# Fused attention and snake MLP on one core: the start of batch 0 regrouped by halves of its heads, and its loads reordered

## The chip, the cores and the metric

The kernel runs on one core of a Trainium2 chip. The metric is device time in microseconds for one launch, inputs and output in the chip's memory. Engines are named as the profile names them: PE is the matrix engine (PEld its weight loads), DVE is VectorE, ACT is ScalarE, POOL is GpSimd, SP is SyncE, which here only issues DMAs. DMAs are issued from the queues of SP, ACT and POOL and run on 16 shared DMA engines.

## The reference

Two stages. A linear attention over 8 batches, 8 heads, 576 tokens and a head dimension of 64, and then a feed-forward layer with a snake activation on the 4608 tokens of width 512.

```python
q_s = np.exp(q - q.max(-1, keepdims=True)); q_s /= q_s.sum(-1, keepdims=True) + 1e-09   # over the head dimension
k_s = np.exp(k - k.max(2, keepdims=True));  k_s /= k_s.sum(2, keepdims=True) + 1e-09    # over the tokens
kv  = np.einsum('bhsd,bhse->bhde', k_s, v)
x   = np.einsum('bhsd,bhde->bhse', q_s, kv)      # -> [4608, 512]
h = x @ w_in                                     # w_in [512, 2048]
s = np.sin(alpha * h)
out = (h + s * s / (alpha + 1e-09)) @ w_out      # w_out [2048, 512]
```

The kernel leaves out the subtraction of the maximum and the small constants, and works in bf16 between f32 inputs and an f32 output.

## The kernel before, in words

**Attention.** One batch is loaded as three tiles of [128, 4, 9, 64] in f32, for q, k and v: a partition is a pair (e, p), head parity and token group; i counts the four pairs of heads; j is one of 9 tokens of a group. A half ii of the heads is the pairs i = ii and ii + 2. Per batch: ACT takes exp of q and k (`exp_q`, `exp_k`, L117); DVE sums and normalises q to qn (`norm_q`, L144 to L146); PE transposes qn to qT (`q_transpose_ii`, L186; DMA transposes in later batches); v is cast to bf16 beside a column of ones (`cast_v0`, L310, for batch 0); PE multiplies k by v over the tokens (`kv_mm`, L157, 18 small matmuls per half); DVE divides by the sums that the column of ones gave, and writes a block-diagonal kbd (`kv_norm`, L167 and L170); PE multiplies kbd by qT (`attn_chunk`, L214), and the result, evacuated from PSUM, is xT, with chunk c of its four belonging to half c // 2.

**Feed-forward.** The 4608 tokens are nine tiles t of 512. For each t and each of 16 column blocks ni, PE computes h from four chunks ki of w_in and xT (`mm_h`, L234), ACT takes the sine (L240), one of ACT, DVE and POOL squares it (L242, L246, L244, by a letter string), and DVE combines s, 1/alpha and h to g in bf16 (`combine`, L250). Then PE multiplies g by w_out (`mm_o`, L254, 64 matmuls of 512 columns per t in four accumulators), and the results are copied (L260) and stored.

**Order.** The order of instructions on each engine is the order of the program text: it is written out by hand, each engine runs its own in order, and waits are semaphores. PSUM is 8 banks: a pool `ps_h` of four one-bank buffers and, during tiles 0 and 1, a pool `ps_e` of two two-bank buffers. Both are rings: a new tile takes the buffer of the one four (or two) before it and waits for its last reader. In tiles 0 and 1 some h come from `ps_e` instead (`lent`): for t = 0 those with ni % 6 in (2, 3). So six h can be in flight.

**The start.** SP issues q and k of batch 0 in halves, v in three parts, and the first 256 columns of w_in in f32 (`st_w`), which POOL later casts to bf16 (L320). POOL waits for the first half of k (`held`, L317) and then issues the rest of w_in with a cast in the DMA, in column blocks (`load_win`, L107), and two quarters of w_out (`load_wout`, L110). PE waits for its data with matmuls that only keep it busy (`warm_up`, L306). Both halves of batch 0 go through exp, norm and transposition, then kv for both, then the four x chunks with their evacuations (L342), a sine on a dummy that loads ACT's table (L343), and h for t = 0. Token group j 8 of batch 0 belongs to tile 1; it is transposed at the start with the others, and its x is computed after ten o matmuls of tile 0 and evacuated by ACT (L393 to L396). `take(os, n)` is: issue the next n o matmuls of the tile before.

Of the kernel before, what the change touches and what calls it, by code (L numbers as in the profile page):

```python
# [23 lines left out]
def kernel(  # L24
# [14 lines left out]
    nc = tc.nc  # L39
# [36 lines left out]
    def src_view(t, b):  # L76
        return t[b].rearrange("(i e) (p j) d -> (e p) i (j d)", e=2, j=J)
# [25 lines left out]

    def load_win(c0, c1):
        n = slice(c0, c1)
        for x in range(2):
            nc.gpsimd.dma_start(out=win[64 * x:64 * x + 64, :, n], in_=win_v[x][:, :, n])  # L107

    def load_wout(c):
        nc.gpsimd.dma_start(out=wout[:, 4 * c:4 * c + 4, :], in_=wout_v[:, 4 * c:4 * c + 4, :])  # L110
# [3 lines left out]

    def exp_to(dst, src):
        for ii in range(2):
            nc.scalar.activation(dst[:, :, ii * 128:(ii + 1) * 128].rearrange("p j (x d) -> p x j d", x=2),  # L117
                                 src[:, ii::2], AX.Exp)

    def exp_q(b):  # L120
        A["qe", b] = att2.tile([128, J, 4 * D], BF16, name="qe")
        exp_to(A["qe", b], staged["q", b])

    def exp_k(b):
        A["ke", b] = att2.tile([128, J, 4 * D], BF16, name="ke")
        exp_to(A["ke", b], staged["k", b])
# [95 lines left out]
    def mm_h(t, ni, wide=None, k0=0, k1=4):  # L222
# [3 lines left out]
        if k0:  # L226
            hp = HP[t, ni]
        elif wide and ni % 6 in ((2, 3) if t == 0 else (4, 5)):
            hp = wide()
        else:  # L230
            hp = ps_h.tile([128, MF], F32, name="hp", tag="h")
# [35 lines left out]
    ACT_CP, DVE_CP, GP_CP = nc.scalar.copy, nc.vector.tensor_copy, nc.gpsimd.tensor_copy  # L267
    V, GP = nc.vector, nc.gpsimd
    nc.scalar.dma_start(out=alpha_rows, in_=moe_alpha.rearrange("(no ni) -> no ni", ni=128))
    load("q", q, 0, halves=True)  # L270
    load("k", k, 0, halves=True)
    staged["v", 0] = st = stage.tile([128, 4, J, D], F32, name="st_v", tag="st")
    VJ = ((0, 0, 9), (1, 0, 5), (1, 5, 9))
    for ii, j0, j1 in VJ:
        nc.sync.dma_start(out=st[:, ii::2, j0:j1].rearrange("p i j d -> p i (j d)"),
                          in_=src_view(v, 0)[:, ii::2, j0 * D:j1 * D])

    wf = stage.tile([128, 4, J, D], F32, name="st_w", tag="st")[:, :, 0:4].rearrange("p c a b -> p c (a b)")
    for x in range(2):
        nc.sync.dma_start(out=wf[64 * x:64 * x + 64], in_=win_v[x][:, :, 0:256])  # L280
    make_identity(nc, ident)
# [10 lines left out]

    tps = [ps_h.tile([128, 8, 128], BF16, name="tp", tag="h") for _ in range(3)]
    warm = ps_h.tile([128, 4, 128], F32, name="warm", tag="h")
# [4 lines left out]

    exp_q(0)  # L300
    exp_k(0)

# [4 lines left out]

    def cast_v0(ii, j0, j1, eng):
        vv = vb[0].rearrange("p j (i c) -> p i j c", i=4)
        eng(vv[:, 2 * ii:2 * ii + 2, j0:j1, 0:D], staged["v", 0][:, ii::2, j0:j1])  # L310


    warm_up(7)
    norm_q(0, [V, V])
    q_tile(0)

    GP_CP(singles.tile([128, 1], F32, name="held"), staged["k", 0][:, 0, 0, 0:1])  # L317
    for c0, c1 in ((256, 512), (512, 1024), (1024, 1536)):
        load_win(c0, c1)
    GP_CP(win[:, :, 0:256], wf)  # L320
    load_win(1536, 2048)
    for c in range(2):
        load_wout(c)
    q_transpose_ii(0, 0, 0, 8, tps[0])
    ACT_CP(A["qT", 0][:, 0, 0:8], tps[0])
    cast_v0(0, 0, 5, ACT_CP)
    cast_v0(0, 5, 9, DVE_CP)
    warm_up(6)
    q_transpose_ii(0, 1, 0, 8, tps[1])
    for ii in range(2):  # L330
        q_transpose_ii(0, ii, 8, 9, tps[2][:, ii:ii + 1])
    cast_v0(1, 0, 5, DVE_CP)
    cast_v0(1, 5, 9, ACT_CP)
    ACT_CP(A["qT", 0][:, 1, 0:8], tps[1])
    ACT_CP(A["qT", 0][:, :, 8], tps[2][:, 0:2])
    for ii in range(2):
        kv_mm(0, ii, ps_e, split=True)
        kv_norm(0, ii, ii + 1)
    for c in range(4):
        xp = ps_h.tile([128, MF], F32, name="hp", tag="h")  # L340
        attn_chunk(0, c, 0, 8, xp)
        (ACT_CP, DVE_CP)[c % 2](xT[:, c, 0:MF], xp)  # L342
    nc.scalar.activation(zero, zero, AX.Sin)  # L343

    def h_slot(t, ni, sq, lag, wide=None):
        hp = mm_h(t, ni, wide, 2 if t < 2 and ni < 2 else 0)
        lag.append((t, ni, hp, sine(t, ni, hp, sq)))
# [26 lines left out]
    with ES:  # L374
        def lent():
# [3 lines left out]
                10: lambda: load_wout(3), 13: lambda: load("k", k, 1, halves=True, gate=DVE_CP)}  # L379
        for ki in range(2):  # L380
            for ni in range(2):
                mm_h(0, ni, lent, ki, ki + 1)
        for ni in range(nN):
# [7 lines left out]
        os = o_quad(0, accs, [DVE_CP, ACT_CP, DVE_CP, ACT_CP])  # L391
        take(os, 10)
        xp = ps_e.tile([128, 4, P], F32, name="xp", tag="a")  # L393
        for c in range(4):
            attn_chunk(0, c, 8, 9, xp[:, c])
        ACT_CP(xT[:, :, 8 * P:9 * P], xp)  # L396
        take(os, 36)
        exp_q(1)
# [169 lines left out]
```

The softmax here doesn't subtract the row's maximum and nothing guards it: scores larger than these inputs give would overflow.

## Time and profile before

| | |
|---|---|
| time, median of 13 runs | 289.76 us (288.81 to 292.38, and one of 491.87) |
| the profiled execution, its own time | 291.86 us |
| its span in the profile | 290.1 us, 4262 instructions |
| mean clock granted to PE | 0.994 |
| first exp (ACT) / first h matmul (PE) / first sine (ACT) | 4.60 / 16.82 / 19.56 us |
| first o matmul (PE) | 32.33 us |
| HBM read and written | 36.71 and 9.44 MB |

The profile is of one execution, and times in it count from the start of its span; its own time is the span and 1.76 us around it. A row of the page is a group of instructions: line, engine, operation, output and inputs with shapes, count, busy time in all and mean of one, then the idle time just before them and what ended most of it. The chain that ended last is followed back from the last instruction.

### The profile page before, as it was taken

Reading aid. Unit: us, or ns where it says so; the run is one execution under the profiler, and the core shown is the slowest. Engines: PE = TensorE matmul, PEld = TensorE weight load, DVE = VectorE, ACT = ScalarE, POOL = GpSimd, SP = SyncE. Lnnn points to the kernel's source line nnn. Section 1 sums busy time; section 2 is a strip of 40 time slices with the busy share of each in tenths; the row PEclk is TensorE's granted clock in tenths of the full one; section 3 lists DMA queues with packets and bytes.
Section 4 is the critical chain, followed back from the end, with each engine's and each line's share of the span. In section 5 each row is a group of like instructions: output and inputs, shape, how many; then the busy total and the mean of one; then the engine's idle time right before and its main releaser. Section 6 shows DMA issues by size and latency. Waiting matters only on the chain.

```text
span 290.1 us, 4262 instructions
## 1 busy us (share of the span) xinstructions
PE 277.4 (96%) x1570; PEld 131.5 (45%) x1570; DVE 188.9 (65%) x280; ACT 227.4 (78%) x321; POOL 79.4 (27%) x73
## 2 busy tenths in 40 slices
PE   2889999999999999999999999999999999999994
PEld 1434445445454445444544454445444444444443
DVE  3847768699958667766777576747674555555412
ACT  4679776899668999899889998899887777777500
POOL 0557720567585743004400350023000000000000
PEclk9979999999999999999999999999999999999999
DMA  7999999963989969019901891115111111111142
GB/s 256 336 204 182 246 362 408 313 251 83 235 120 384 411 216 157 19 26 320 335 21 37 280 368 32 37 38 118 36 38 36 36 36 38 36 36 37 40 108 72
DMA packets 37893, 46.03 MB, mean 159 GB/s; under 512 B 15968, under 2 KB 21360, under 8 KB 37872
## 3 DMA queue, kind: packets, MB, share of 16 engines
q1 hardware_dynamic: 33392, 41.69, 47.6%
q0 software_dynamic: 4288, 3.93, 8.5%
q8 instruction: 12, 0.20, 0.3%
q10 hardware_dynamic: 192, 0.14, 0.2%
q14 instruction: 9, 0.07, 0.1%
HBM read 36.71 MB, written 9.44 MB: 159 GB/s over the span
## 4 chain that ended last, share of the span: by engine, by line
PE 83%; DMA 5%; POOL 4%; DVE 3%; SPq 1%; issue 1%; ACT 1%; POOLq 0%
PE hp L234 36%; PE op L254 34%; PE hp L254 4%; DMA st_w<-in_moe_w_in_dram 4%; POOL s L244 3%; PE kvp L157 2%; PE xp L206 2%; PE hh L234 2%; DMA qT<-qn 1%; PE op L538 1%; PE op L234 1%; ACT s L240 1%; DVE g L250 1%; DVE qs L144 1%; SPq L94 1%
## 5 line engine op out<-in xcount | busy, mean ns | idle before, releaser
L250 DVE SCALAR_TENSOR_TENSOR g<-s,inva_sb,hp 128x512 bf16<-128x512 f32 x130 | 96.2, 746 | 64.4 <-ACT s L242 54.2
L234 PE MATMUL hp<-xT,win 128*128 128x512 bf16 x520 | 131.4, 383 | 0.6 <-POOL win L320 0.6
L254 PE MATMUL op<-wout,g 128*128 128x512 bf16 x496 | 124.2, 379 | 0.0
L240 ACT ACTIVATE s<-hp,alpha_sb 128x512 f32<-128x512 f32 x130 | 87.8, 682 | 27.0 <-PE hp L234 25.8
L234 PEld LDWEIGHTS <-win 128*128 128x128 bf16 x576 | 56.7, 99 | 69.4 <-issue 2.4
L254 PEld LDWEIGHTS <-g 128*128 128x128 bf16 x560 | 54.1, 98 | 61.9 <-issue 1.0
L242 ACT ACTIVATE s<-s 128x512 f32<-128x512 f32 x112 | 70.5, 630 | 3.5
L146 POOL TENSOR_TENSOR qn<-qe,qs 128x1152 bf16<-128x1152 bf16 x12 | 25.3, 2128 | 73.8 <-DVE qs L140 62.8
L244 POOL TENSOR_TENSOR s<-s 128x512 f32<-128x512 f32 x29 | 30.5, 1061 | 24.0 <-ACT s L240 23.3
L260 DVE COPY o<-op 128x512 f32<-128x512 f32 (+2 forms) x33 | 22.1, 669 | 9.9 <-PE op L254 7.5
L117 ACT ACTIVATE ke<-st_k 128x1152 bf16<-128x1152 f32 x16 | 17.9, 1151 | 3.2 <-DMA st_k<-in_k_dram 3.2
L117 ACT ACTIVATE qe<-st_q 128x1152 bf16<-128x1152 f32 x16 | 17.8, 1156 | 2.5 <-DMA st_q<-in_q_dram 2.4
L139 DVE TENSOR_REDUCE qs<-qe 128x36 f32<-128x2304 bf16 x5 | 12.8, 2553 | 8.7 <-ACT qe L117 8.6
L131 POOL CAST vb<-st_v 128x1152 bf16<-128x1152 f32 x12 | 13.6, 1163 | 10.5 <-DMA st_v<-in_v_dram 6.9
L254 PE MATMUL hp<-wout,g 128*128 128x512 bf16 x64 | 15.1, 379 | 0.0
L209 DVE CAST xT<-xp 128x512 bf16<-128x512 f32 (+1 forms) x18 | 13.4, 743 | 0.0
L144 DVE TENSOR_REDUCE qs<-qe 128x18 f32<-128x1152 bf16 x6 | 8.0, 1331 | 4.4 <-ACT qe L117 4.4
L157 PE MATMUL kvp<-vb,ke 64*128 64x130 bf16 x288 | 10.0, 216 | 0.8 <-ACT vb L310 0.8
L157 PEld LDWEIGHTS <-ke 64*128 64x128 bf16 x288 | 8.3, 93 | 4.4 <-issue 1.8
L117 ACT ACT_TABLE_LOAD x7 | 9.0, 1283 | 1.3 <-PEq L552 1.2
L234 PE MATMUL hh<-xT,win 128*128 128x512 bf16 x40 | 9.5, 381 | 0.0
L206 PE MATMUL xp<-qT,kbd 128*128 128x256 bf16 (+1 forms) x40 | 8.2, 286 | 0.4 <-DVE xT L209 0.3
(68 smaller groups left out, 117.5 us busy)
## 6 DMA issues: line engine op xcount, KB each, us to landing
out_dram<-o SPq DMA_DIRECT2D x70, 128.0 KB, 2.4
st_q<-in_q_dram SPq DMA_DIRECT2D x6, 1152.0 KB, 6.3
st_k<-in_k_dram SPq DMA_DIRECT2D x6, 1152.0 KB, 8.4
st_v<-in_v_dram SPq DMA_DIRECT2D x6, 1152.0 KB, 10.2
st_q<-in_q_dram SPq DMA_DIRECT2D x4, 576.0 KB, 4.5
st_k<-in_k_dram SPq DMA_DIRECT2D x4, 576.0 KB, 7.3
wout<-in_moe_w_out_dram POOLq DMA_DIRECT2D x4, 512.0 KB, 9.2
st_v<-in_v_dram SPq DMA_DIRECT2D x3, 576.0 KB, 9.1
```

The lines of the kernel that those rows point to most:

```text
L117: nc.scalar.activation(dst[:, :, ii * 128:(ii + 1) * 128].rearrange("p j (x d) -> p x j d", x=2), src[:, ii::2], AX.Exp)
L131: engs[ii](vv[:, 2 * ii:2 * ii + 2, :, 0:D], staged["v", b][:, ii::2])
L146: engs[ii % len(engs)].tensor_tensor(qn[:, ii].rearrange("p j (x d) -> p j x d", x=2), qe[:, ii], part.unsqueeze(3).to_broadcast([128, J, ...
L157: nc.tensor.matmul(kvp[:, e, ii * 130:(ii + 1) * 130], ke[r, j, ii * 128:(ii + 1) * 128], vt[r, j, ii * 130:(ii + 1) * 130], start=(j == 0 ...
L206: nc.tensor.matmul(xp[:, e, 0:n], kt[:, e, ii], qT[:, ii, j0:j1, e * 64:(e + 1) * 64], start=True, stop=True)
L234: nc.tensor.matmul(hp, win[:, ki, ni * 128:(ni + 1) * 128], xT[:, ki, t * MF:(t + 1) * MF], start=(ki == 0), stop=(ki == 3))
L240: nc.scalar.activation(s, hp, AX.Sin, scale=alpha_sb[:, ni:ni + 1])
L242: nc.scalar.activation(s, s, AX.Square)
L244: nc.gpsimd.tensor_tensor(s, s, s, op=ALU.mult)
L250: nc.vector.scalar_tensor_tensor(G[t][:, ni], in0=s, scalar=inva_sb[:, ni:ni + 1], in1=hp, op0=ALU.mult, op1=ALU.add)
L254: nc.tensor.matmul(acc, G[t][:, ni, j * 128:(j + 1) * 128], wout[:, ni, :], start=(ni == 0), stop=(ni == nN - 1))
L260: eng(o[:, cols], acc)
```

## The change

The loads of batch 0 are issued in another order and from other queues: SP issues the first halves of q and k, the second half of q and the first half of v; POOL, as soon as the first half of q has landed, issues the second halves of k and v, and then all of w_in in blocks of 512 columns, the first of these in two halves of its rows. The f32 columns of w_in and their cast are gone. POOL casts the first half of v, between two of its requests.

Batch 0 then runs by halves of the heads. Exp goes q, k, q, k by halves; kv, normalisation and x chunks 0 and 1 of the first half come before kv of the second. Chunk 0 of h for the first four ni is issued before x chunks 2 and 3 are computed; those two share one `ps_e` tile and are both evacuated by DVE; chunk 1 of four ni and chunk 2 of three ni follow. The first four h of t = 0 are therefore all in `ps_h`, and the lent ones are those with ni % 6 in (4, 5) in both tiles.

Token group j 8 of batch 0 is transposed after ten o matmuls of tile 0 and its qT copied by ACT; after ten more its x is computed, and DVE evacuates it.

```diff
@@ -101,10 +101,10 @@
         load("k", k, b)
         load("v", v, b)
 
-    def load_win(c0, c1):
+    def load_win(c0, c1, ks=slice(0, 4)):
         n = slice(c0, c1)
         for x in range(2):
-            nc.gpsimd.dma_start(out=win[64 * x:64 * x + 64, :, n], in_=win_v[x][:, :, n])
+            nc.gpsimd.dma_start(out=win[64 * x:64 * x + 64, ks, n], in_=win_v[x][:, ks, n])
 
     def load_wout(c):
         nc.gpsimd.dma_start(out=wout[:, 4 * c:4 * c + 4, :], in_=wout_v[:, 4 * c:4 * c + 4, :])
@@ -112,14 +112,19 @@
 
     A = {}
 
-    def exp_to(dst, src):
-        for ii in range(2):
+    def exp_to(dst, src, iis=range(2)):
+        for ii in iis:
             nc.scalar.activation(dst[:, :, ii * 128:(ii + 1) * 128].rearrange("p j (x d) -> p x j d", x=2),
                                  src[:, ii::2], AX.Exp)
 
     def exp_q(b):
         A["qe", b] = att2.tile([128, J, 4 * D], BF16, name="qe")
         exp_to(A["qe", b], staged["q", b])
+
+    def exp_half(name, b, ii):
+        if ii == 0:
+            A[name + "e", b] = att2.tile([128, J, 4 * D], BF16, name=name + "e")
+        exp_to(A[name + "e", b], staged[name, b], (ii,))
 
     def exp_k(b):
         A["ke", b] = att2.tile([128, J, 4 * D], BF16, name="ke")
@@ -225,7 +230,7 @@
             G[t] = gpool.tile([128, nN, MF], BF16, name="g")
         if k0:
             hp = HP[t, ni]
-        elif wide and ni % 6 in ((2, 3) if t == 0 else (4, 5)):
+        elif wide and ni % 6 in (4, 5):
             hp = wide()
         else:
             hp = ps_h.tile([128, MF], F32, name="hp", tag="h")
@@ -266,18 +271,16 @@
 
     ACT_CP, DVE_CP, GP_CP = nc.scalar.copy, nc.vector.tensor_copy, nc.gpsimd.tensor_copy
     V, GP = nc.vector, nc.gpsimd
+    for n in "qkv":
+        staged[n, 0] = stage.tile([128, 4, J, D], F32, name=f"st_{n}", tag="st")
+
+    def load0(eng, n, t, ii, j0=0, j1=J):
+        eng.dma_start(out=staged[n, 0][:, ii::2, j0:j1].rearrange("p i j d -> p i (j d)"),
+                      in_=src_view(t, 0)[:, ii::2, j0 * D:j1 * D])
+
+    for n, t, ii in (("q", q, 0), ("k", k, 0), ("q", q, 1), ("v", v, 0)):
+        load0(nc.sync, n, t, ii)
     nc.scalar.dma_start(out=alpha_rows, in_=moe_alpha.rearrange("(no ni) -> no ni", ni=128))
-    load("q", q, 0, halves=True)
-    load("k", k, 0, halves=True)
-    staged["v", 0] = st = stage.tile([128, 4, J, D], F32, name="st_v", tag="st")
-    VJ = ((0, 0, 9), (1, 0, 5), (1, 5, 9))
-    for ii, j0, j1 in VJ:
-        nc.sync.dma_start(out=st[:, ii::2, j0:j1].rearrange("p i j d -> p i (j d)"),
-                          in_=src_view(v, 0)[:, ii::2, j0 * D:j1 * D])
-
-    wf = stage.tile([128, 4, J, D], F32, name="st_w", tag="st")[:, :, 0:4].rearrange("p c a b -> p c (a b)")
-    for x in range(2):
-        nc.sync.dma_start(out=wf[64 * x:64 * x + 64], in_=win_v[x][:, :, 0:256])
     make_identity(nc, ident)
     DVE_CP(identb, ident)
     zero = singles.tile([128, 1], F32, name="zero")
@@ -290,60 +293,80 @@
     ES = ExitStack()
     ps_e = ES.enter_context(tc.tile_pool(name="ps_e", bufs=2, space=PSUM, reuse_waits="tile"))
 
-    tps = [ps_h.tile([128, 8, 128], BF16, name="tp", tag="h") for _ in range(3)]
+    tp0 = ps_h.tile([128, 8, 128], BF16, name="tp", tag="h")
     warm = ps_h.tile([128, 4, 128], F32, name="warm", tag="h")
     tpa = warm[:, 0, 0:nN]
     nc.tensor.transpose(tpa, alpha_rows, ident[0:nN, 0:nN])
     DVE_CP(alpha_sb, tpa)
     nc.vector.reciprocal(inva_sb, alpha_sb)
 
-    exp_q(0)
-    exp_k(0)
-
-    def warm_up(n):
-
-        for _ in range(n):
-            nc.tensor.matmul(warm, identb, A["qe", 0][:, 0:4, 0:128], start=True, stop=True)
+
 
     def cast_v0(ii, j0, j1, eng):
         vv = vb[0].rearrange("p j (i c) -> p i j c", i=4)
         eng(vv[:, 2 * ii:2 * ii + 2, j0:j1, 0:D], staged["v", 0][:, ii::2, j0:j1])
 
-
+    GP_CP(singles.tile([128, 1], F32, name="held"), staged["q", 0][:, 0, 0, 0:1])
+    load0(GP, "k", k, 1)
+    load0(GP, "v", v, 1, 0, 5)
+    load0(GP, "v", v, 1, 5, 9)
+    load_win(0, 512, slice(0, 2))
+    cast_v0(0, 0, 9, GP_CP)
+    load_win(0, 512, slice(2, 4))
+    for c0 in (512, 1024, 1536):
+        load_win(c0, c0 + 512)
+    for c in range(2):
+        load_wout(c)
+
+    def warm_up(n):
+
+        for _ in range(n):
+            nc.tensor.matmul(warm, identb, A["qe", 0][:, 0:4, 0:128], start=True, stop=True)
+
+
+
+
+    exp_half("q", 0, 0)
+    exp_half("k", 0, 0)
+    exp_half("q", 0, 1)
     warm_up(7)
     norm_q(0, [V, V])
     q_tile(0)
-
-    GP_CP(singles.tile([128, 1], F32, name="held"), staged["k", 0][:, 0, 0, 0:1])
-    for c0, c1 in ((256, 512), (512, 1024), (1024, 1536)):
-        load_win(c0, c1)
-    GP_CP(win[:, :, 0:256], wf)
-    load_win(1536, 2048)
+    q_transpose_ii(0, 0, 0, 8, tp0)
+    ACT_CP(A["qT", 0][:, 0, 0:8], tp0)
+    exp_half("k", 0, 1)
+    warm_up(2)
+    kv_mm(0, 0, ps_e, split=True)
+    warm_up(3)
+    kv_norm(0, 0, 1)
+    tp1 = ps_e.tile([128, 8, 128], BF16, name="tp", tag="a")
+    q_transpose_ii(0, 1, 0, 8, tp1)
+    cast_v0(1, 0, 5, ACT_CP)
+    cast_v0(1, 5, 9, DVE_CP)
+
+    def x_chunk(c, xp, eng):
+        attn_chunk(0, c, 0, 8, xp)
+        eng(xT[:, c, 0:MF], xp)
+
     for c in range(2):
-        load_wout(c)
-    q_transpose_ii(0, 0, 0, 8, tps[0])
-    ACT_CP(A["qT", 0][:, 0, 0:8], tps[0])
-    cast_v0(0, 0, 5, ACT_CP)
-    cast_v0(0, 5, 9, DVE_CP)
-    warm_up(6)
-    q_transpose_ii(0, 1, 0, 8, tps[1])
-    for ii in range(2):
-        q_transpose_ii(0, ii, 8, 9, tps[2][:, ii:ii + 1])
-    cast_v0(1, 0, 5, DVE_CP)
-    cast_v0(1, 5, 9, ACT_CP)
-    ACT_CP(A["qT", 0][:, 1, 0:8], tps[1])
-    ACT_CP(A["qT", 0][:, :, 8], tps[2][:, 0:2])
-    for ii in range(2):
-        kv_mm(0, ii, ps_e, split=True)
-        kv_norm(0, ii, ii + 1)
-    for c in range(4):
-        xp = ps_h.tile([128, MF], F32, name="hp", tag="h")
-        attn_chunk(0, c, 0, 8, xp)
-        (ACT_CP, DVE_CP)[c % 2](xT[:, c, 0:MF], xp)
+        x_chunk(c, ps_h.tile([128, MF], F32, name="hp", tag="h"), (ACT_CP, DVE_CP)[c])
+    kv_mm(0, 1, ps_e, split=True)
+    kv_norm(0, 1, 2)
+    ACT_CP(A["qT", 0][:, 1, 0:8], tp1)
     nc.scalar.activation(zero, zero, AX.Sin)
+    for ni in range(4):
+        mm_h(0, ni, None, 0, 1)
+    xp = ps_e.tile([128, 2, MF], F32, name="xp", tag="a")
+    for e in range(2):
+        x_chunk(2 + e, xp[:, e], DVE_CP)
+    for ni in range(4):
+        mm_h(0, ni, None, 1, 2)
+    for ni in range(3):
+        mm_h(0, ni, None, 2, 3)
 
     def h_slot(t, ni, sq, lag, wide=None):
-        hp = mm_h(t, ni, wide, 2 if t < 2 and ni < 2 else 0)
+        done = 3 if t == 0 and ni < 3 else 2 if (t, ni) == (0, 3) or t == 1 and ni < 2 else 0
+        hp = mm_h(t, ni, wide, done)
         lag.append((t, ni, hp, sine(t, ni, hp, sq)))
 
     def flush(lag, keep):
@@ -377,9 +400,6 @@
 
         late = {6: lambda: load("q", q, 1, halves=True, gate=DVE_CP), 8: lambda: load_wout(2),
                 10: lambda: load_wout(3), 13: lambda: load("k", k, 1, halves=True, gate=DVE_CP)}
-        for ki in range(2):
-            for ni in range(2):
-                mm_h(0, ni, lent, ki, ki + 1)
         for ni in range(nN):
             h_slot(0, ni, "DPAPPAPPAPPAPPAP"[ni], lag, lent)
             flush(lag, 1)
@@ -390,11 +410,16 @@
         accs = [ps_h.tile([128, dm], F32, name="hp", tag="h") for _ in range(4)]
         os = o_quad(0, accs, [DVE_CP, ACT_CP, DVE_CP, ACT_CP])
         take(os, 10)
+        tp = ps_e.tile([128, 2, 128], BF16, name="tp", tag="a")
+        for ii in range(2):
+            q_transpose_ii(0, ii, 8, 9, tp[:, ii:ii + 1])
+        ACT_CP(A["qT", 0][:, :, 8], tp)
+        take(os, 10)
         xp = ps_e.tile([128, 4, P], F32, name="xp", tag="a")
         for c in range(4):
             attn_chunk(0, c, 8, 9, xp[:, c])
-        ACT_CP(xT[:, :, 8 * P:9 * P], xp)
-        take(os, 36)
+        DVE_CP(xT[:, :, 8 * P:9 * P], xp)
+        take(os, 26)
         exp_q(1)
         load("v", v, 1, halves=True)
         load_batch(2)
```

More of the change, by code (lines that the diff above doesn't have):

```diff
@@ L298, with cast_v0 @@
     nc.vector.reciprocal(inva_sb, alpha_sb)
-    exp_q(0)
-    exp_k(0)
+    def cast_v0(ii, j0, j1, eng):
+        vv = vb[0].rearrange("p j (i c) -> p i j c", i=4)
+        eng(vv[:, 2 * ii:2 * ii + 2, j0:j1, 0:D], staged["v", 0][:, ii::2, j0:j1])
+    GP_CP(singles.tile([128, 1], F32, name="held"), staged["q", 0][:, 0, 0, 0:1])
[9 more added lines that the diff above has]
+        load_wout(c)
     def warm_up(n):
@@ L306, in warm_up @@
             nc.tensor.matmul(warm, identb, A["qe", 0][:, 0:4, 0:128], start=True, stop=True)
-    def cast_v0(ii, j0, j1, eng):
-        vv = vb[0].rearrange("p j (i c) -> p i j c", i=4)
-        eng(vv[:, 2 * ii:2 * ii + 2, j0:j1, 0:D], staged["v", 0][:, ii::2, j0:j1])
+    exp_half("q", 0, 0)
+    exp_half("k", 0, 0)
+    exp_half("q", 0, 1)
     warm_up(7)
```

## The prediction

> **What bounds the kernel now.** I read the page first, for the chain that ended last and PE's share. PE is 96% busy and carries 83% of the chain, so the program is a PE stream with an idle beginning.
>
> ```profile
> PE 277.4 (96%) x1570; PEld 131.5 (45%) x1570; DVE 188.9 (65%) x280; ACT 227.4 (78%) x321; POOL 79.4 (27%) x73
> ...
> PE 83%; DMA 5%; POOL 4%; DVE 3%; SPq 1%; issue 1%; ACT 1%; POOLq 0%
> ```
>
> Then PE's waits from 30 us to the end: three waits of 0.3 us. Whatever PE gains or loses before about 37 us therefore reaches the end one to one; nothing behind it can take it up or pay for it.
>
> ```profile
> PE hp L214 <- DMA qT<-qn: 0.3, 1, 0.3
> PE xp L206 <- DVE xT L209: 0.3, 1, 0.3
> PE xp L214 <- DVE g L250: 0.3, 1, 0.3
> ```
>
> The timeline of the first 36 us (start, length, instruction) shows both ends of the first h block: PE is let go at 16.82 by the cast of w_in's f32 columns; the first sine starts at 19.56; the 16 sines and their squares end at 33.59 (32.92 + 0.67); PE starts the first ten o matmuls at 32.33, while the last combines (DVE, L250) still run.
>
> ```profile
> 8.34 1.16 ACT L117 ACTIVATE ke<-st_k 128x1152 bf16<-128x1152 f32 x1 [1.09 <-DMA st_k<-in_k_dram]
> ...
> 15.72 1.04 POOL L320 CAST win<-st_w 128x1024 bf16<-128x1024 f32 x1 [3.01 <-DMA st_w<-in_moe_w_in_dram]
> ...
> 16.82 3.55 PE L234 MATMUL hp<-xT,win 128*128 128x512 bf16 x8 [0.56 <-POOL win L320]
> ...
> 19.56 0.69 ACT L240 ACTIVATE s<-hp,alpha_sb 128x512 f32<-128x512 f32 x1 [1.37 <-PE hp L234]
> ...
> 32.33 2.41 PE L254 MATMUL hp<-wout,g 128*128 128x512 bf16 x10
> ...
> 34.22 1.40 DVE L250 SCALAR_TENSOR_TENSOR g<-s,inva_sb,hh 128x512 bf16<-128x512 f32 x2
> ...
> 35.02 0.28 PE L214 MATMUL xp<-qT,kbd 128*128 128x64 bf16 x4 [0.28 <-DVE g L250]
> ```
>
> Stretches of 3.41 us show PE's clock (stretch, length, busy of PE, PEld, DVE, ACT, POOL, then the clock). PE was busy 1.68 us in the first and ran at half clock in the next: eight matmuls at 0.427 us instead of 0.2155.
>
> ```profile
> 13.54:16.95 3.41, 1.68 (x14) 0.56 (x13) 2.59 (x7) 3.14 (x6) 1.23 (x2) 0.99 1.31 205
> 16.95:20.36 3.41, 3.41 (x9) 1.22 (x8) 0.12 (x2) 1.91 (x3) 2.49 (x4) 0.51 1.23 203
> ```
>
> The DMA queues from 12 to 13 us, one line each: GpSimd's queue (q0) moved next to nothing although its first w_in request was issued at 8.83. It starts when SP's queue (q1) runs dry.
>
> ```profile
> q1 hardware_dynamic: 242, 0.23, 110.9%
> q0 software_dynamic: 10, 0.01, 3.7%
> ```
>
> **What the skill says.** "TensorE: Matmul & The Clock Gate", Part 1: the clock halves after an idle window of about 3.4 us and returns after a busy one, and the windows run freely. The trace agrees: half clock from 16.93 to 20.33; and it shows that a window need not be empty (49% busy was too little, 2.92 of 3.41 us in the window before was enough). "DMA: Bandwidth & Descriptors", Queues, rings and completion order: the DMA engines go round-robin between queues. The trace differs; its queues are served nearly in order of request, and I go by the trace. "GPSIMD Engine Reference", Key points: GpSimd shares its SBUF interfaces with VectorE; the L146 multiply took 1.97 us beside GpSimd at 41.4 against 1.36 alone.
>
> **The loads.** SP now asks for four halves (qa, ka, qb, va; a and b are the halves of batch 0's heads). Before, the first four requests landed at 4.55, 6.05, 8.3 and 9.7 (starts of the exps they release, and issue plus landing), so ka comes at 6.05, but qb at 8.3, 2.2 later than before. GpSimd's copy waits for qa, 4.6 to 5.1, then issues kb, two parts of vb and two of w_in at 0.65 each (3.88 for 6), to 8.4. Their data follows SP's: 0.59 MB per half at 0.40 MB/us gives kb near 10.5, vb by 12, the first half of w_in's rows near 13.3. The f32 columns went at 0.23 MB/us, so dropping them shortens the stream by about a microsecond. GpSimd's cast of va (1.16, row L131) replaces that of the columns (1.04) and runs 9.75 to 10.9; queued behind it are eight w_in and two w_out issues, 8 x 0.65 + 2 x 0.77 = 6.7, to 17.6. The issues also wait for the landings of those eight back, all of them earlier. GpSimd's first square comes at 19.5: free.
>
> **The start, in order.** ACT: exp qa to 5.76, ka to 7.25, qb 8.35 to 9.5, qT copy to 10.75 (0.99), exp kb to 11.9, vb cast to 12.65. DVE: qa's sums and product as before, to 8.85; qb's take 1.35 + 0.27 + 1.36 with gaps, 9.55 to 12.6. PE's kv of half a is done by 11.7 (va 10.9, 18 matmuls 0.7), but its normalisation (L167, L170: 0.8) stands behind qb on DVE: 13.4. Then x chunks 0 and 1 on PE to 14.05; DVE's vb cast 14.05 and xT 14.75; ACT's xT 14.5, qT 15.55, table load 16.85. kv of half b ends at 14.7, its normalisation, behind DVE's xT, at 15.6. PE does four h matmuls from 14.7, x 2 and 3 to 16.2, and four and three more. DVE evacuates both x chunks, 2 x 0.68, to 17.45; the matmul with chunk 3 follows PE's seven, 17.75 to 17.97, and the first sine starts at **18.1** instead of 19.56. Bounds: 17.3 if qb lands 0.8 sooner (even spacing of 1.5 after 6.05), 19 if vb or w_in come a microsecond late. The added warm-ups (12 for 13) fill PE waits and cost nothing. PE has 12 h matmuls done then, where before it had 5 or 6.
>
> **The h block.** ACT is the limit: from the third sine (21.31) to the end of the last (33.59) it never waits, 12.28 us. The third would start 1.4 after the first, so the block ends 18.1 + 13.68 = 31.8: 1.8 earlier than in the profile. PE's further lead (52 matmuls left, 11.2 us) is worth nothing, because each h needs the buffer of six earlier.
>
> **The tail, which gives it back.** The lent buffers move from ni 2, 3 (mod 6) to 4, 5. The four accumulators of the o matmuls took the buffers of h 10, 11, 12, 13; now they take 12, 13, 14, 15. Against the end of the last sine (zero), combine 12 ends at -0.27, 13 at +0.72, 14 at 1.3, 15 at 2.0 (rows at 32.57, 33.56, 34.22). The first o matmul runs, the second waits for combine 13, and everything queues behind it: seven more to +2.25, two to +2.7, two transposes of j 8 (0.12), ten more to 4.97, the j 8 chunk to 5.25; 44 o matmuls remain. Before, ten and the chunk were done at +1.71, and 44 remained at 1.71 + 10 x 0.2155 = 3.87. So 1.4 is lost. Late: 18.1 + 13.68 + 5.25 = 37.03 against 37.46. The moved j 8 pieces (ACT 0.38, DVE 0.37) lie beside PE's o matmuls; exp of batch 1 starts at about 36.4, against 37.02, and PE reaches its transposes at 42.7, as before. Sum without the clock: **-0.4**.
>
> **The clock in that tail.** h 15 needs combine 9 (3.1 before the last sine's end), so PE finishes it near -2.2 and has one matmul until +0.72: about 2.7 us idle in 2.9. Most positions of a 3.41 us window leave PE less busy there than the 49% that cost half clock. The half-clock stretch of 3.41 then falls mostly on o matmuls: at most 1.7 lost, at least 0; I take 1.2. Sum: **+0.8** on the profiled execution, 291.86 (span 290.1 and 1.76 around it): 292.6. That execution is 2.1 above the median, 289.76. Warm at 16.9, its first sine would come at 18.3 and the block would end 1.6 earlier, at about 290.2; some runs will have been so. That leaves 0.5 above the median unexplained; taking it off, the forecast is **292.0**.
>
> **Rivals.** (1) The same tail, but the clock stays full: -0.4, or about 290.8 on the same footing. For it: the window's phase differs by run, and its threshold is known only to lie between 49% and 86%. (2) The queues share after all, or PE is cold while it does the first h matmuls: qb lands near 9.8, DVE's chain is 1.5 late, first sine 19.3 to 19.6: 293.3. Against it: GpSimd's queue moved 0.01 MB while SP's was busy. (3) Faster: the first sine comes at 17.3, because qb is not held up as the third request was, and the tail stays warm: 1.2 below the profiled time, 290.7, and taken from the median 288.5; from a first sine before 17.1 it is over 0.5% faster. For it: six GpSimd requests and the slow columns no longer crowd the stream. Against: DVE's serial chain, 9.55 to 17.45, has hardly a gap. (4) That the order is not what the diff says, I exclude for the h block: queue and buffers follow from the code.
>
> **The numbers.** Forecast 45%, rival 1 25%, rival 2 17%, rival 3 13%. A change within 0.5% (1.45 us) can't be told from none here. Slower: most of the forecast (40), rival 2 (17), a little of rival 1 (3): 0.60. Same: the rest of the forecast, most of rival 1, part of rival 3: 0.30. Faster: 0.10. Range 289.0 to 293.4, from half of rival 3 to rival 2.
>
> **What would show it.** Right: first sine near 18.1; the second o matmul waiting for DVE's g at about 32.5; PE idle near 30 to 32.5, then half clock for 3.4 us. Wrong: qb's exp later than 8.6 (sharing), PE cold at the first h matmuls, no idle before the o matmuls, or a w_out landing that PE waits for.

## The result, and the profile after

The changed kernel takes 291.78 us (median of 11 runs, 290.53 to 292.66) against 289.71 for the kernel before: ratio 1.0064 [1.0041, 1.0086], 2.07 us slower. The forecast was 292.0 and slower. The size is right, but by luck: the trace shows that two of its terms were wrong, one against the other. The profiled execution took 292.28 us, with a span of 290.5.

The page, engine totals and shares of the chain that ended last:

```profile
PE 275.5 (95%) x1569; PEld 130.2 (45%) x1569; DVE 189.1 (65%) x281; ACT 225.8 (78%) x318; POOL 82.5 (28%) x78
...
PE 86%; DMA 6%; POOL 4%; ACT 1%; DVE 1%; issue 1%; SPq 1%
```

PE is busy 1.9 us less than in the profile before, mostly because none of its matmuls ran at half clock, and yet the span is 0.4 longer: PE now waits more. PE's waits of this kernel (total, times, longest, all in us), those that are new:

```profile
PE hp L239 <- DMA win<-in_moe_w_in_dram: 1.2, 1, 1.2
PE hh L239 <- DMA win<-in_moe_w_in_dram: 0.9, 1, 0.9
PE hp L259 <- DVE st_k L89: 0.9, 1, 0.9
PE xp L219 <- DVE xT L349: 0.8, 1, 0.8
...
PE hp L259 <- DVE g L255: 0.6, 1, 0.6
```

Two of the five were in the prediction: the two o matmuls at L259 (L254 before). The first of them is named after L89, two one-column copies that DVE did beside it; what PE waited for is combine 12, which ended at 32.95. Two waits for w_in and one for an x chunk were not in it. The timeline (start, length, instruction, idle before and its releaser) shows where they lie:

```profile
8.07 1.16 ACT L117 ACTIVATE qe<-st_q 128x1152 bf16<-128x1152 f32 x1 [0.71 <-DMA st_q<-in_q_dram]
...
16.39 0.38 PE L219 MATMUL xp<-qT,kbd 128*128 128x512 bf16 x1 [0.78 <-DVE xT L349]
...
16.81 0.69 DVE L349 CAST xT<-xp 128x512 bf16<-128x512 f32 x1 [0.47 <-PE xp L219]
...
18.84 1.89 PE L239 MATMUL hp<-xT,win 128*128 128x512 bf16 x8 [1.21 <-DMA win<-in_moe_w_in_dram]
...
19.90 1.84 ACT L245 ACTIVATE s<-hp,alpha_sb 128x512 f32<-128x512 f32 x3 [3.37 <-PE hp L239]
...
21.60 1.90 PE L239 MATMUL hh<-xT,win 128*128 128x512 bf16 x8 [0.88 <-DMA win<-in_moe_w_in_dram]
...
32.56 0.67 ACT L245 ACTIVATE s<-hp,alpha_sb 128x512 f32<-128x512 f32 x1
...
33.00 0.38 PE L259 MATMUL hp<-wout,g 128*128 128x512 bf16 x1 [0.87 <-DVE st_k L89]
...
34.00 2.10 PE L259 MATMUL hp<-wout,g 128*128 128x512 bf16 x9 [0.62 <-DVE g L255]
...
38.21 0.28 PE L219 MATMUL xp<-qT,kbd 128*128 128x64 bf16 x4
```

Up to the last x chunk the start keeps to the forecast: qb's exp at 8.07 (8.35 forecast), the last evacuation's end at 17.50 (17.45). Then the second half of w_in's rows is missing until 18.84, and the first sine comes at 19.90 instead of 18.1. The sines end at 33.23, and 44 o matmuls are left at 38.49, 5.26 after it (forecast 5.25). That is 1.0 later than in the profile before; 0.4 of it is gone at 79 us, where the earlier kernel loses 0.3 on its transposes (L214).

The clock, by stretches (length, busy time of PE, PEld, DVE, ACT, POOL, then the clock, DMA share and GB/s):

```profile
28.90:32.30 3.40, 3.24 (x15) 1.37 (x14) 2.37 (x5) 3.25 (x6) 3.38 (x5) 1.00 1.10 339
32.30:35.70 3.40, 2.08 (x9) 0.87 (x9) 2.84 (x6) 0.94 (x2) 1.91 (x2) 1.00 1.21 220
```

Having waited for w_in until 21.60, PE has no lead over ACT: it does its last 48 h matmuls without a pause (10.5 us) and ends them at 32.14, 1.1 before the last sine's end, not the 2.2 forecast. It idles only 0.87 and 0.62 us before the two o matmuls, and the clock stays at 1.00.

Why w_in is late in this execution shows in the DMA queues. GpSimd's queue (packets, MB written, time of the packets as a share of 16 engines) from 13 to 14 us and from 14 to 15, when nothing else is moving:

```profile
q0 software_dynamic: 133, 0.12, 91.7%
...
q0 software_dynamic: 127, 0.12, 96.8%
```

The same kind of request ran at 0.20 MB a microsecond in the kernel before (207 packets and 123.4% from 16 to 17 us, much the same to 20). Here fewer packets are under way, and they take longer: 91.7% of 16 us over 133 packets is 0.110 us each, against 0.095 there; single ones take up to 1.29 us. From 12 to 17 us the queue moves 0.18 + 0.12 + 0.12 + 0.10 + 0.12 = 0.64 MB, 0.36 less than at 0.20 a microsecond.

### The profile page after: what moved, and what is told of

The parts are those of the page before. It is cut to its first block, busy times and chain, and to the rows that moved or that the text cites. A ratio compares the mean times of both kernels' runs of the same rounds, so it can differ in the third digit from the quotient of the medians.

```text
span 290.5 us, 4257 instructions
## 1 busy us (share of the span) xinstructions
PE 275.5 (95%) x1569; PEld 130.2 (45%) x1569; DVE 189.1 (65%) x281; ACT 225.8 (78%) x318; POOL 82.5 (28%) x78
## 4 chain that ended last, share of the span: by engine, by line
PE 86%; DMA 6%; POOL 4%; ACT 1%; DVE 1%; issue 1%; SPq 1%
PE op L259 37%; PE hp L239 35%; PE hp L259 5%; DMA win<-in_moe_w_in_dram 3%; PE kvp L162 3%; POOL s L249 2%; DMA st_v<-in_v_dram 2%; PE hh L239 2%; PE xp L211 2%; PE op L563 1%; PE op L239 1%; ACT s L245 1%; POOL win L107 1%; DVE g L255 1%; SPq L278 1%
## 5 line engine op out<-in xcount | busy, mean ns | idle before, releaser
L255 DVE SCALAR_TENSOR_TENSOR g<-s,inva_sb,hp 128x512 bf16<-128x512 f32 x132 | 97.5, 746 | 64.4 <-ACT s L247 54.2
L259 PE MATMUL op<-wout,g 128*128 128x512 bf16 x496 | 124.2, 379 | 0.0
L245 ACT ACTIVATE s<-hp,alpha_sb 128x512 f32<-128x512 f32 x132 | 88.9, 682 | 28.9 <-PE hp L239 27.6
L239 PEld LDWEIGHTS <-win 128*128 128x128 bf16 x576 | 56.0, 98 | 70.7 <-issue 3.0
L259 PEld LDWEIGHTS <-g 128*128 128x128 bf16 x560 | 54.1, 98 | 63.0 <-issue 2.6
L259 PE MATMUL hp<-wout,g 128*128 128x512 bf16 x64 | 15.2, 379 | 1.5 <-DVE st_k L89 0.9
L214 DVE CAST xT<-xp 128x512 bf16<-128x512 f32 (+1 forms) x18 | 13.4, 743 | 0.0
L239 PE MATMUL hh<-xT,win 128*128 128x512 bf16 x32 | 7.6, 379 | 0.9 <-DMA win<-in_moe_w_in_dram 0.9
```

What stands on the lines that cost most here:

```text
L239: nc.tensor.matmul(hp, win[:, ki, ni * 128:(ni + 1) * 128], xT[:, ki, t * MF:(t + 1) * MF], start=(ki == 0), stop=(ki == 3))
L245: nc.scalar.activation(s, hp, AX.Sin, scale=alpha_sb[:, ni:ni + 1])
L255: nc.vector.scalar_tensor_tensor(G[t][:, ni], in0=s, scalar=inva_sb[:, ni:ni + 1], in1=hp, op0=ALU.mult, op1=ALU.add)
L259: nc.tensor.matmul(acc, G[t][:, ni, j * 128:(j + 1) * 128], wout[:, ni, :], start=(ni == 0), stop=(ni == nN - 1))
```

## The experiments

Theory, after the result: (1) the tail costs about 1.4 us because of the lent buffers; (2) the late first sine comes from w_in's landing, out of GpSimd's queue; (3) had the first sine come in time, PE would have idled at the tail and the clock would have halved. Rivals: the tail costs nothing by itself; the queue is slow because of a neighbour on the chip (DVE, f32 loads in the same queue, the place read in memory) rather than of when its requests are issued.

**1. The tail alone.** The kernel before with the new lent buffers and nothing else:

```
-        elif wide and ni % 6 in ((2, 3) if t == 0 else (4, 5)):
+        elif wide and ni % 6 in (4, 5):
```

> The kernel before with one part of the change alone: for t = 0 the lent h buffers are ni % 6 in (4, 5). Theory (the tail gives back): the accumulators of the o matmuls then take the buffers of h 12 to 15, so the second o matmul waits for combine 13 and PE stands idle before 33 us; the 44 last o matmuls begin 1.0 to 1.4 us later against the end of the last sine, and the time grows by 1.0 to 1.4 us, up to 2.8 if PE's clock halves after the idle time. Rival (the order of buffers is nothing, the loss of the change is all in w_in's late landing): within 0.3 us of the kernel before.

290.81 us against 290.06, ratio 1.0029 [1.0013, 1.0045]. PE's waits of this kernel:

```profile
PE hp L254 <- DVE g L250: 1.5, 2, 0.9
```

Both waits are there, 0.88 and 0.61 us before the first and second o matmul. The tail by itself makes the kernel slower by 0.8 us (0.4 to 1.3), a little under what was expected; the rival that it costs nothing falls.

**2. The tail taken back out of the changed kernel,** by lending two more tiles, so that the accumulators take earlier buffers:

```
-        elif wide and ni % 6 in (4, 5):
+        elif wide and (ni % 6 in (4, 5) or t == 0 and ni > 13):
```

> The changed kernel with h 14 and 15 of t = 0 lent as well, so that the accumulators take the buffers of h 8, 9, 12, 13 and the first eight o matmuls wait for no late combine. Theory: PE is busy from 32.1 on, the idle 1.5 us before the o matmuls go; h 14 and 15 now wait for combines 10 and 11 and the last sine ends up to 0.5 later; the time falls by 0.6 to 1.1 us against the changed kernel (about 290.8). Rival: the tail is nothing, 291.8 or above.

291.49 us, 1.0056 [1.0043, 1.0069]: no gain that its interval tells from the changed kernel's, so the expected 0.6 to 1.1 us didn't come. The timeline of ACT says why:

```profile
31.45 0.69 ACT L245 ACTIVATE s<-hh,alpha_sb 128x512 f32<-128x512 f32 x1 [1.04 <-PE hh L239]
```

h 14 now waits for a lent tile (PE 0.80, for DVE's g), and the sine after it for PE: 1.04 us. The wait went from the o matmuls into the h block: it was moved, not removed.

This run says something of the loads too, since its start is the changed kernel's. GpSimd's queue was as slow (0.13, 0.12, 0.06 and 0.09 MB from 13 to 17 us), yet PE did its first twelve h matmuls without waiting for w_in, and waited 0.95 only for columns 512 on. The first sine came at 19.01, not 19.90.

**3. Is DVE in the way of GpSimd's queue?** In the changed kernel DVE works through the slow stretch, in the kernel before it was idle when w_in loaded. Three casts are added to the kernel before, in that idle time; their result is not used:

```
+    scratch = singles.tile([128, 2, J, D], BF16, name="scratch")
+    for _ in range(3):
+        DVE_CP(scratch, staged["v", 0][:, 0::2])
```

> The kernel before with three casts of 128x1152 f32 to bf16 added on VectorE at about 17.0 to 19.3 us, where it was idle while GpSimd issued four w_in and w_out requests and its queue moved 0.20 MB/us. Theory (GpSimd writing its requests beside VectorE's work slows its queue): the queue moves 0.12 to 0.15 MB/us there and its packets get up to 1 us long, as in the changed kernel from 12 to 18 us. Rival (nothing of VectorE's slows the queue): 0.20 MB/us as before.

290.11 us in a single run, span 288.3. The queue from 17 to 18 and from 18 to 19 us, beside DVE's casts (17.28 to 19.75):

```profile
q0 software_dynamic: 213, 0.20, 123.1%
...
q0 software_dynamic: 216, 0.21, 125.5%
```

Nothing is lost beside these casts, and this rival falls. The run serves twice: its clock was 1.00 throughout, so it shows the kernel before without its half-clock stretch. The first sine comes at 18.54, the last ends at 32.12.

**4. Are the f32 loads in GpSimd's queue in the way of w_in?** kb and vb go to SP's queue:

```
-    load0(GP, "k", k, 1)
-    load0(GP, "v", v, 1, 0, 5)
-    load0(GP, "v", v, 1, 5, 9)
+    load0(nc.sync, "k", k, 1)
+    load0(nc.sync, "v", v, 1, 0, 5)
+    load0(nc.sync, "v", v, 1, 5, 9)
```

> The changed kernel with the second halves of k and v requested by SP's queue as before; GpSimd's first request is w_in's. Theory (GpSimd's issuing beside VectorE slows its queue): the six w_in requests after the cast of v are still issued at 11 to 16 us, the queue still moves about 0.12 MB/us from 12 to 17, and the first sine stays at 19.3 to 20. Rival (f32 loads and casting loads in one software queue are what is slow): 0.20 MB/us from 12 on, the second half of w_in's first rows lands by 15.5 and the first sine starts near 18.1.

292.58 us, 1.0089 [1.0061, 1.0117]. GpSimd's queue is no better for it: it moved 0.05 MB from 12 to 14 us in each microsecond, 0.13, 0.07 and 0.09 in the next three, and the first sine came at 20.77. This rival falls too. The time is 0.8 us above the changed kernel's, though the two intervals overlap. The queues weren't served in order of request here: all of SP's loads had been requested before w_in, but from 10 to 12 us GpSimd's queue moved 0.07 and 0.09 MB while SP's, not yet done, moved 0.11 and 0.16.

**5. Is the first access to a row slow?** Two loads of one column each, on ACT's queue, touch every row of w_in at the start:

```
+    touch = singles.tile([128, 4, 1], F32, name="touch")
+    for x in range(2):
+        nc.scalar.dma_start(out=touch[64 * x:64 * x + 64], in_=win_v[x][:, :, d_ff - 1:d_ff])
```

> The changed kernel with two small loads on ACT's queue at the start that read the last element of each of w_in's 512 rows. Theory F (the first read of w_in's rows is slow, whoever makes it, and later reads of the same rows are not): GpSimd's queue moves 0.20 MB/us from 12 us on without long packets, w_in's second half of rows lands by 15.5, the first sine starts near 18.1, and the time falls by 0.8 to 1.5 us against the changed kernel. Rivals (the shape of the requests, or the columns): 0.12 MB/us from 13 to 17 as before and 291.8.

291.53 us, 1.006 [1.0046, 1.0075]. From 12 to 14 us the queue ran at 0.19 to 0.20, but from 14 on it fell to 0.13, 0.09 and 0.12. PE waited 0.92 for w_in (columns 512 on); the first sine came at 18.78. First access can't be the whole cause. The time can't be told from the changed kernel's, 291.78, although this first sine is 1.1 us earlier.

**6. Other columns, other requests.** Two single runs of the changed kernel. In one, every block of columns is read from the place of the block before it; in the other, the first 512 columns come in two requests instead of four, both ahead of GpSimd's cast:

```
-            nc.gpsimd.dma_start(out=win[64 * x:64 * x + 64, ks, n], in_=win_v[x][:, ks, n])
+            nc.gpsimd.dma_start(out=win[64 * x:64 * x + 64, ks, n], in_=win_v[x][:, ks, (c0 + 1536) % 2048:(c0 + 1536) % 2048 + c1 - c0])
```

```
-    load_win(0, 512, slice(0, 2))
+    load_win(0, 512)
     cast_v0(0, 0, 9, GP_CP)
-    load_win(0, 512, slice(2, 4))
```

> The changed kernel with each block of 512 columns of w_in taken from the block before it (the first from columns 1536 to 2047), so h is of other columns than alpha and w_out belong to; the work is the same. Theory C (columns 0 to 511 are slow to read): 0.20 MB/us from 12 to 17 us, and the slow stretch comes with the second block, at 14 to 18. Theory F or S: slow from 12 or 13 to 17 as before.

> The changed kernel with w_in's first 512 columns requested in two loads of 64x4x512, both before the cast of v, in place of four of 64x2x512. Theory S (the half shape is slow): 0.20 MB/us from 12 us on. Theory F or C (first touch of the rows, or the columns 0 to 511): still about 0.12 MB/us from 13 to 17. By order alone the rows of chunks 2 and 3 land some 1.5 us sooner, the others later.

With other columns: 291.00 us, slow from 13 to 16 us as before (0.13, 0.11, 0.12), so the place in memory is not the cause. Here too PE didn't wait for the second half of the rows, only 0.49 us for columns 512 on, and the first sine came at 18.43. With whole rows: 297.25 us. The queue was slow from 12 to 13 (0.15) and then ran at 0.18 to 0.21 from 13 on, in the very stretch that was slow in the changed kernel. But the first h matmul waited 1.10 us for all four row blocks, PE cooled, and half clock ran from 17.1 to 24 and again in the tail: the first sine came at 23.07. This points to how and when the requests are issued; their shape and their order were changed together here.

**7. All four row requests ahead of the cast,** the smallest such edit, in a single run and then timed:

```
     load_win(0, 512, slice(0, 2))
-    cast_v0(0, 0, 9, GP_CP)
     load_win(0, 512, slice(2, 4))
+    cast_v0(0, 0, 9, GP_CP)
```

> The changed kernel with the third and fourth w_in request issued ahead of the cast of v. If the queue is slow because GpSimd issues while it moves, the stretch of long packets begins later or is shorter, as only six requests follow the cast; if it is slow for what it reads, it stays from 12 to 17 us at 0.12 MB/us. The first sine then comes within 0.5 us of 19.9.

> The changed kernel with w_in's third and fourth request ahead of the cast of v, timed. Theory: w_in is in time and the first sine comes at 18.6 in place of 19.9, but PE then waits 2.3 us for combines 12 and 13 and its clock halves in a part of the runs; the median is no better than the changed kernel's by more than 0.8 us: 291.0 to 292.4. Rival (w_in's landing is all that the change loses): 290.2 or below.

292.54 us in the single run; timed 292.64, 1.0086 [1.0056, 1.0115]. The queue is slow from 12 to 13 us only, PE waits 0.21 us at most for w_in, the first sine comes at 18.60 in the one and 18.56 in the other (the first expectation, within 0.5 of 19.9, missed), and the kernel is still no faster. The six executions fall into two groups: two at 291.21 with clock 1.000, four at 292.60 to 292.99 with 0.994. The timed run's waits, timeline and stretches show what happens:

```profile
PE hp L259 <- DVE g L255: 2.3, 2, 1.6
```

```profile
31.57 0.38 PE L259 MATMUL hp<-wout,g 128*128 128x512 bf16 x1 [1.64 <-DVE g L255]
32.57 3.79 PE L259 MATMUL hp<-wout,g 128*128 128x512 bf16 x9 [0.62 <-DVE g L255]
```

```profile
29.00:32.80 3.80, 1.54 (x8) 0.51 (x7) 3.27 (x7) 2.43 (x4) 3.71 (x4) 1.00 1.16 288
32.80:36.20 3.40, 3.40 (x10) 1.19 (x9) 1.03 (x2) 0.00 (x0) 0.05 (x1) 0.50 1.20 226
36.20:39.60 3.40, 3.40 (x22) 1.69 (x21) 0.64 (x2) 3.06 (x4) 0.00 (x0) 1.00 1.05 398
```

PE is done early with h 15, idles 1.64 + 0.62 us, is busy 1.54 of 3.80, and the next 3.40 us run at half clock: ten matmuls where the stretch after it holds 22. That is the forecast's tail, in this kernel instead of the changed one. The two groups differ by 1.4 to 1.8 us, near the forecast's bound of 1.7.

**8. The same, but with later requests.** Three copies on GpSimd (3.13 us, result not used) stand between the cast and the six later w_in requests:

```
     cast_v0(0, 0, 9, GP_CP)
+    idle = singles.tile([128, J, D], F32, name="idle")
+    for _ in range(3):
+        GP_CP(idle, staged["q", 0][:, 0])
```

> The same kernel with three copies of 128x576 on GpSimd (about 1.8 us) after the cast, so that the six later w_in requests go out 1.8 us later. Theory G (a request that the engines reach less than some 3 us after its issue runs with long packets): the queue falls to 0.10 to 0.14 MB/us with packets of 0.3 to 1 us at 14 to 17. Rival (the slow stretch belongs to the first rows read, whenever they come): 0.20 MB/us while it has requests.

291.21 us in a single run. The queue ran dry from 15.0 to 15.4, and then the late requests, issued at 13.69 to 17.39, were served soon after. From 16 to 17 us here, and in the same microsecond of the timed run of 7, whose requests were issued from 10.64 on:

```profile
q0 software_dynamic: 124, 0.13, 86.9%
```

```profile
q0 software_dynamic: 217, 0.21, 125.6%
```

Requests of the same shape and size, and 0.13 MB for 0.21; what was changed is the time from issue to service. This speaks for the reading (theory G) that requests which the engines reach soon after their issue, here within some 3 us, run slowly, and it fits the changed kernel, where the cast holds the third request back until 10.63 and the fifth until 11.79, and the slow stretch begins at 13. Its rival, that only the first rows are slow, falls, and so does a slowing by GpSimd's issuing itself: in 7 it issued from 13.89 to 16.70 while the queue moved 0.20 to 0.21. But the age of a request and the number of requests that wait change together in these runs, and which of the two counts wasn't tested. Nor is it the whole: from 12 to 13 us the requests issued some four microseconds before were slow in 7 (0.09 MB) and not in 5 (0.20). The mechanism stays open.

The waits before the o matmuls are those of 7 (1.65 and 0.62 us), yet the clock stayed at 1.00; the account below comes back to this.

**9. The halves without their faults.** On top of 7: the lent buffers of batch 0 as in the kernel before, and x chunks 2 and 3 in two tiles instead of one. In the first version ACT evacuates chunk 2 ahead of its table load; in the second DVE evacuates both. The rest of the edit, not shown, only hands the lent buffers on.

```
-        elif wide and ni % 6 in (4, 5):
+        elif wide and ni % 6 in ((2, 3) if t == 0 else (4, 5)):
...
-    nc.scalar.activation(zero, zero, AX.Sin)
-    for ni in range(4):
-        mm_h(0, ni, None, 0, 1)
-    xp = ps_e.tile([128, 2, MF], F32, name="xp", tag="a")
+    xps = [ps_h.tile([128, MF], F32, name="hp", tag="h") for _ in range(2)]
+    for ni in range(2):
+        mm_h(0, ni, lent, 0, 1)
     for e in range(2):
-        x_chunk(2 + e, xp[:, e], DVE_CP)
+        x_chunk(2 + e, xps[e], (ACT_CP, DVE_CP)[e])
+    nc.scalar.activation(zero, zero, AX.Sin)
+    for ni in (2, 3):
+        mm_h(0, ni, lent, 0, 1)
```

> The changed kernel with four edits: w_in's first four requests ahead of the cast of v; x chunks 2 and 3 in two one-bank buffers in place of one shared tile, chunk 2 evacuated by ACT ahead of its table load; h 2 and 3 of t = 0 lent as in the kernel before, so that the accumulators take the buffers of h 10 to 13. Theory (the change's start is good for something once w_in lands in time and the o matmuls don't wait): first sine at 17.7, last sine's end at about 31.1, no half clock before the o matmuls, 44 o matmuls left at 35.1 against 36.0 in an execution of the kernel before at full clock; 288.6 to 289.2 us, 0.2 to 0.4% faster than before. Rival (another limit holds the start, or w_in comes late again): 289.7 or above.

> As the run before it but with both x chunks evacuated by VectorE and ACT's table load where the change has it. Theory: first sine at 18.2 to 18.6, no PE idle of more than 0.5 us before the o matmuls, full clock; 289.3 to 290.0 us, the same as the kernel before within 0.2%. Rival (the tail is nothing): no faster than the run with w_in's rows first, 291.5 or above.

The first: 289.69 us against 289.71, 1.0006 [0.9985, 1.0027]. Its first sine comes at 17.92 and 44 o matmuls are left near 35.1, 0.9 earlier than in run 3, the undisturbed kernel before. The expected gain of 0.5 to 1.1 us is lost again in batch 1. ACT's timelines of the first version, then of run 3 (exp of the second half of k, cast of v):

```profile
40.96 1.16 ACT L117 ACTIVATE ke<-st_k 128x1152 bf16<-128x1152 f32 x1 [1.74 <-DVE qn L151]
42.47 1.17 ACT L136 CAST vb<-st_v 128x1152 bf16<-128x1152 f32 x1 [0.35 <-DMA st_v<-in_v_dram]
```

```profile
40.65 1.16 ACT L117 ACTIVATE ke<-st_k 128x1152 bf16<-128x1152 f32 x1 [0.46 <-DMA st_k<-in_k_dram]
42.02 1.17 ACT L131 CAST vb<-st_v 128x1152 bf16<-128x1152 f32 x1 [0.21 <-DMA st_v<-in_v_dram]
```

SP requested these loads 1.0 us earlier than in run 3 (k's second half at 31.45 for 32.45), but they landed no earlier: k's 9.4 us after its request for 8.1, at 40.85 for 40.55. (The first row names DVE; k's own landing is 0.1 before it.) So ACT's lead is gone at 41 us, the first sine of tile 1 starts at 50.18 against 50.13, and PE's lead, 0.9 at 41 us, is down to 0.01 at 62.4. At 77 us both versions and run 3 stand together (77.28, 77.33 and 77.35 at the same group of o matmuls). Why the loads took longer was not tested. Later, at 175.86, the first version waited 0.8 us for a DMA transpose; that is part of why its profiled execution, 290.82, lies 1.1 above its median.

The second version: 289.45 us, 0.9985 [0.9973, 0.9998], with its first sine at 18.53 and clocks of 0.997 to 1.000 in all 22 runs. It is the best of the kernels here, 0.15% faster than the kernel before, and far under the 0.5% below which the prediction claimed nothing.

## Why the prediction was right in time, and where it was wrong

One table holds the account: of single executions, the first sine's start, the last sine's end, the execution's own time and what is left of it after the last sine (the third from the second).

| kernel | first sine | last sine's end | own time | left |
|---|---|---|---|---|
| before, undisturbed (3) | 18.54 | 32.12 | 290.11 | 257.99 |
| second version of 9 | 18.53 | 31.72 | 289.90 | 258.18 |
| after | 19.90 | 33.23 | 292.28 | 259.05 |
| touched rows (5) | 18.78 | 32.15 | 291.16 | 259.01 |
| late requests (8) | 18.83 | 32.02 | 291.21 | 259.19 |
| before, new lent buffers (1) | 18.34 | 31.92 | 291.34 | 259.42 |
| after, two more lent (2) | 19.01 | 33.37 | 291.68 | 258.31 |
| rows ahead of the cast (7) | 18.56 | 31.74 | 292.81 | 261.07 |
| other columns (6) | 18.43 | 31.62 | 291.00 | 259.38 |
| first version of 9 | 17.92 | 31.09 | 290.82 | 259.73 |

The last column falls into three: 258.0 to 258.3 with the earlier tail or with two more tiles lent, 259.0 to 259.4 with the new one at full clock, 261.1 with the new one at half clock. The last row stands outside: it has the earlier tail, but lost its lead of 1.0 us in batch 1 and 0.8 at 175.86.

- **The tail: right in kind, place and size.** Combine 12 at -0.28 (forecast -0.27), the second o matmul at +0.77 (+0.72), 44 left at +5.26 (+5.25). Of these 1.4 us about 1.0 reaches the end: 1.1 by the table, 0.8 in the timed run 1. That whatever PE loses before 37 us reaches the end one to one was a little too strict.
- **The loads: wrong, and this is the step that failed.** The stream's rate was taken as a property of the bytes: "the first half of w_in's rows near 13.3", and the rest at the speed that the trace before showed. The first half did come in time; in the profiled execution the second came 1.2 us after PE wanted it. How late it comes differs from one execution to the next: with the same order of loads and the same slow stretch, 2 and the other columns of 6 didn't wait for it, and had their first sines at 19.01 and 18.43. The rule that queues are served nearly in order of request held here, from 9 to 10 us, where GpSimd's queue moved 0.40 MB and SP's four packets; in 4 it did not.
- **The first sine, 19.9 for 18.1.** Where w_in is there (7) it comes at 18.56. So 1.34 of the 1.8 is the landing. The other 0.46 is a wait that was overlooked: x chunks 2 and 3 lie in one tile, and the second x matmul waits 0.78 us for DVE's evacuation of the first, where the forecast let both run by 16.2. In 9, with two tiles and ACT's help, it is 17.92; with two tiles alone the wait is gone too, but in that execution the second half of k came late (its exp at 11.97 for 11.15), and the first sine with it, 18.53.
- **The clock: 1.2 us put in, nothing came.** The mechanism is real, run 7 shows it and its price of 1.4 to 1.8 us; but it needs PE to be far ahead of ACT, and its idle time to fall into one window (below), and in the profiled execution the late w_in took that lead away. In none of the changed kernel's timed runs did the mean clock fall under 0.998. Thus the two errors hide each other, and that the sum came near 292 is luck. What the late w_in costs at the end is less sure than its 1.3 us at the first sine: in the timed runs the two executions of 7 at full clock took 291.21, 0.6 below the changed kernel's median, and the touched rows 0.25 below it. With the half-clock executions 7 is 0.9 above it. So of the 2.07 us the tail's 0.8 is shown by timed runs, and how the rest divides is not.
- **The footing: right.** The profiled execution before was one with half clock (mean 0.994); the executions at that clock in these comparisons took 291.4 to 291.9, the others had a median of 289.7 to 290.0. Against run 3 the change is 1.36 later at the first sine and 1.06 longer after the last, with 0.25 regained between: 2.17, the whole difference of the two executions, 292.28 and 290.11.

Of the rivals, the first (the same tail, full clock, 290.8) named the clock rightly and missed the time by the late w_in; the second had the first sine (19.3 to 19.6) and the time (293.3) nearly, but for a cause that wasn't there, since qb landed early and PE was warm at the first h matmuls. The third did not occur.

"TensorE: Matmul & The Clock Gate", Part 1, of the Trainium skill, on which the clock term rests, speaks of an idle window, and of windows that run freely. These traces agree with the second: until PE's work ends, every stretch of half or full clock in them is a whole multiple of 3.413 us (half clock for 3.413 in the kernel before and in 7, for 6.827 with the whole rows of 6), so each trace shows where its windows lie. The windows that hold the tail in 7 (timed), in 8 and with the other columns of 6, with the columns of the stretches above:

```profile
29.38:32.80 3.42, 1.16 (x6) 0.36 (x5) 2.90 (x7) 2.05 (x4) 3.33 (x4) 1.00 1.18 276
```

```profile
27.61:31.02 3.41, 2.60 (x13) 1.08 (x11) 2.42 (x4) 3.06 (x6) 3.39 (x5) 1.00 1.16 281
31.02:34.43 3.41, 1.95 (x9) 0.84 (x9) 2.94 (x6) 1.00 (x2) 2.04 (x2) 1.00 1.14 287
```

```profile
29.63:33.04 3.41, 1.62 (x8) 0.58 (x6) 2.89 (x7) 1.89 (x3) 3.02 (x3) 1.00 1.15 288
```

In 7 both waits fall into one window and half clock follows; in 8 the same waits are split over two, and it doesn't. In the changed kernel they are 1.49 us together, so no window there is busy for less than 1.92 us of 3.41, and 1.92 in one window of run 1 left the clock full. How much is enough these runs do not settle: half clock followed 1.16, 1.46, 1.47, 1.49 and 1.68 us busy, and did not follow 1.62 (above) and 1.64 (the changed kernel from 15.82 to 19.24). So the 49% that the prediction took from one window is not a threshold.

## What to carry to other kernels

Before pricing an idle stretch of an engine, ask which of its earlier waits would use up the lead that makes it idle: a late load and a cold clock are not two costs to be added. Where the clock goes by windows, ask too how the stretch may lie across them. When buffers are lent in a circle, count which tiles the next consumer takes over and when those were released; that count gave the tail to a few hundredths here. A lead won at the start is worth only what the next arrival leaves of it (here the landing of batch 1's k and v took 0.9 us), so find that arrival first. And one profile is one execution: with the same order of loads the first sine came at 18.43, 19.01 and 19.90.

## What was not expected of the hardware

- GpSimd's casting loads of w_in have two speeds in one kernel, with nothing else on the DMA engines: 0.20 to 0.21 MB written a microsecond, and 0.10 to 0.13, with fewer packets under way and single ones of up to 1.29 us. DVE's casts beside it make no difference (3), nor does the place in memory (6), nor is it only the first access (5). Requests reached soon after issue were slow in 8; whether it is that or the number of them that wait, and why those of 7 were slow from 12 to 13 us, wasn't settled.
- Moving two casting requests ahead of a 1.2 us cast (7) came with a first sine 1.3 us before that of the changed kernel's profiled execution, and with a clock window at half speed in four of six runs.
